# Two small transfers of an attention kernel, begun by ScalarE instead of SyncE from step 84 on

## The chip, the cores and the metric

The kernel runs on one core of a Trainium2 chip. The time is that of the device for one execution, in microseconds: 2188.83 us in the median of three runs before the change (2188.59 to 2190.87). Engines are named as the profile names them: PE is TensorE, PEld its weight loads, DVE is VectorE, ACT is ScalarE, POOL is GpSimd, SP is SyncE. Each engine works off its own queue of instructions in program order; an instruction that waits holds up everything behind it in that queue. A transfer (DMA) is begun by an instruction in the queue of some engine, and lands later.

## The reference, cut to what matters

```python
def _A_ref(x, wqkv, wo):                       # x: 1 x 2048 x 640
    H = 32; Dh = D // H; W = 256
    q, k, v = split((x @ wqkv).reshape(B, S, 3, H, Dh))
    scores = einsum("bhqd,bhkd->bhqk", q, k) * Dh ** -0.5
    mask = (idx[:, None] - idx[None, :] >= 0) & (idx[:, None] - idx[None, :] < W)
    p = softmax(where(mask, scores, -1e9))
    return einsum("bhqk,bhkd->bhqd", p, v).reshape(B, S, D) @ wo

def _B_ref(x, dft_seq_re, dft_seq_im, dft_hid_re, dft_hid_im):
    a = x @ dft_hid_re.T
    b = x @ dft_hid_im.T
    return dft_seq_re @ a - dft_seq_im @ b

x = x + _A_ref(_layernorm(x), A_wqkv, A_wo)
x = x + _B_ref(_layernorm(x), ...)
x = x + _A_ref(_layernorm(x), A_wqkv, A_wo)
x = x + _B_ref(_layernorm(x), ...)
```

Two attention layers with a window of 256 keys alternate with two Fourier layers. The change touches the attention layers alone, and both in the same way.

## The kernel before

An attention layer has 32 heads, taken in eight quads of four. Sixteen blocks of 128 positions times eight quads are 128 steps, which `heads` (L606) writes out in one order by hand. In step n it issues, for three different places in the sequence:

- **t**, place n: `t_pair` (L655) multiplies keys by queries for two heads at a time, so scores come out transposed, keys on the partitions (L659). The queries carry an extra row with the negated maximum of each query, and the keys a row of ones, so the maximum is subtracted within the product. `t_exp` (L663) takes the exponential on ScalarE (L669, twice a step: z = 0 and z = 1, two heads each), `t_mask` (L672) clears what lies outside the window on GpSimd (L675, L679).
- **s**, place n + 10: `s_head` (L626) makes the plain scores (L631), and VectorE adds the mask and takes each query's maximum (L636). For every four blocks `m_rows` (L641) transposes the maxima on TensorE (L644), ScalarE writes them negated to the tile `mt` (L647), and two transfers (L649) put them into the extra rows of the query tile `qp`. That happens in the steps 4k + 2, and the rows are wanted by L659 four steps later.
- **v**, place n - 1: `pv` (L685) multiplies the exponentials by the values (L694); a column of ones among the values gives the sum of each row. ScalarE copies the result to `ou` (L701). After every fourth block `finish` (L705) sends the row sums to the tile `sm` (L711) and the whole of `ou` to memory (L712), VectorE takes the reciprocals (L714), and they are sent to memory too (L717).

Scores live in banks of PSUM that are lent for a stretch of time by a plan (`borrow`, L139, and `borrow_pair`, L147, with the numbers HELD_T, HELD_S and HELD_PV). A bank that L669 hasn't read yet can't be written by the next L659, L631 or L694.

Between these products TensorE gets other work as filling: the projection of later quads (L257, then stored to `qk_d`, L524) and, when that is done, parts of the output product. Loads of head rows from `qk_d` into `kp` and `qp` (L594, twelve for each four blocks) are issued some four steps ahead of their use. Other loads are those of values (L621), of finished heads (L859) and their reciprocals (L865), of x (L951).

What matters for the change is who issues a transfer, and when. `post(delay, fn)` (L169) puts a function off by some ticks; there are two ticks a step (`tick`, L175, called at L829 after each z). A delay of 1 from within a half-step runs at that half-step's own end. So the two transfers of L649 are issued directly behind L647 in program order. The row sums have a delay of 2 in the first seven quads, which is the end of the next step's first half, behind that half's L669; in the last quad it is 1, directly behind L701. The reciprocal comes at a delay of 9, or 5 in the last quad. All transfers of the kernel are begun by SyncE, in the order in which they are issued.

Of the kernel before, what the change touches and what calls it, by code (L numbers as in the profile page):

```python
# [15 lines left out]
P = 128  # L16
# [5 lines left out]
NQ = H // 4  # L22
# [13 lines left out]
FIRST = 7  # L36
LATE = 9
BACK = 2
PACE = 0.65

STEP = 2.5
# [23 lines left out]
class Net:  # L65
# [89 lines left out]
    def next(self, name):  # L155
        i = self.turn.get(name, 0)
        self.turn[name] = i + 1
        tiles = getattr(self, name)[:3]
        return tiles[i % len(tiles)]
# [422 lines left out]
    def pack(self, quad, sb):  # L582
# [20 lines left out]
                    todo.append(lambda d=dst[b:b + 20, :, cols], src=src: put(d, src))  # L603
        return todo

    def heads(self, xsrc, xdst, hook):  # L606
        nc = self.nc
        qp = [t.rearrange("p (z s) -> p z s", z=2) for t in self.qp]
# [32 lines left out]
        def m_rows(quad, u, bank):  # L641
            m = mc.pop((quad, u))
            p = self.banks[:16, bank, 3 * P:]
            nc.tensor.transpose(p, m.rearrange("p z e j -> p (z e j)"), self.ident)  # L644
            mt = pool.tile([16, P], F32R, name="mt", tag="mt", bufs=1)
            yield
            nc.scalar.activation(mt, p, AF.Copy, scale=-1.0)  # L647
            for z in range(2):
                self.post(1, lambda z=z: nc.sync.dma_start(  # L649
                    qp[quad % 2][60:125:64, z, u * 512:(u + 1) * 512].bitcast(F32),  # L650
                    mt[8 * z:8 * z + 8, :].bitcast(F32)))

# [32 lines left out]
        def pv(quad, qb, bank):  # L685

            bk, at = qb // 4, qb % 4 * P
            if qb % 4 == 0:
                ous[quad, bk] = self.next("ou")
            for kb in range(max(qb - 2, 0), qb + 1):  # L690
                t = pt[quad, kb]
                vq = self.vq[(4 * quad + kb // 4) % 3]
                for h in range(4):
                    nc.tensor.matmul(  # L694
                        self.banks[32 * h:32 * h + 32, bank, :P],
                        vq[:, 96 * (kb % 4) + 21 * h:96 * (kb % 4) + 21 * h + 32],
                        t[:, h, (qb - kb) * P:(qb - kb + 1) * P],
                        start=kb == max(qb - 2, 0), stop=kb == qb,
                        tile_position=(0, 32 * h), skip_group_check=True)
            pt.pop((quad, qb - 2), None)  # L700
            nc.scalar.activation(ous[quad, bk][:, at:at + P], self.banks[:, bank, :P], AF.Copy)  # L701
            if qb % 4 == 3:
                finish(quad, bk)

        def finish(quad, bk):  # L705
            ou = ous.pop((quad, bk))
            sm = pool.tile([P, 16], F32, name="sm", tag="sm")
            rc = pool.tile([P, 16], F32, name="rc", tag="rc")
            cols = slice(bk * 512, (bk + 1) * 512)
            at = (2, 9, 11) if quad < NQ - 1 else (1, 5, 6)  # L710
            self.post(at[0], lambda: nc.sync.dma_start(sm, ou[0:P:32, :]))  # L711
            self.post(at[0], lambda: nc.sync.dma_start(  # L712
                self.od[4 * quad:4 * quad + 4, :, cols].rearrange("h r s -> (h r) s"), ou))
            self.post(at[1], lambda: nc.vector.reciprocal(out=rc, in_=sm))  # L714

            def store():
                nc.sync.dma_start(  # L717
                    self.rd[bk, 4 * quad:4 * quad + 4, :].rearrange("h (a b) -> (h a) b", b=16), rc)
                self.post(2 if quad < NQ - 1 else 0, lambda: self.stored.add((quad, bk)))
            self.post(at[2], store)  # L720
# [17 lines left out]
        def more():  # L738
# [5 lines left out]
            if not self.left:  # L744
                if self.part_t < NB - BACK:
                    self.now = self.out if self.ready_part() else None
                else:
                    self.now = self.rest if self.late_t < BACK and self.ready_late() else None
            return next(self.now, None) if self.now else None
# [26 lines left out]
        for step in range(-LEAD, steps + 1):  # L776
# [28 lines left out]
            for z in range(2):  # L805
                if 0 <= t < steps:
                    banks = self.borrow_pair(clock + AT_T[z], HELD_T)
                    t_pair(t // 16, t % 16, z, banks)
                if 0 <= s < steps:
                    for e, b in enumerate(self.borrow(clock + AT_S[z], *HELD_S)):  # L810
                        s_head(s // 16, s % 16, 2 * z + e, b)
                if z and (rows or 0 <= v < steps):
                    last, = self.borrow(clock + AT_PV, HELD_PV)
                m = m_rows(*rows, last) if z and rows else iter(())
                next(m, None)
                if 0 <= t < steps:
                    t_exp(t // 16, t % 16, z, banks)
                    t_mask(t // 16, t % 16, z)
                if self.heavy:
                    self.heavy.sort(key=lambda h: h[0] not in ROLES["m"])  # L820
                    self.relieve()
                if z:
                    if 0 <= v < steps:
                        pv(v // 16, v % 16, last)
                    for _ in m:
                        pass
                if z == 0 or t < -1 or t >= steps:
                    fill(nf)
                self.tick()  # L829
# [274 lines left out]
    def spend(self, us):  # L1104
        self.spent += us
        while self.spent >= PACE:
            self.spent -= PACE
            self.tick()
# [756 lines left out]
```

## Time and profile before

| | |
|---|---|
| median of three runs | 2188.83 us |
| the profiled execution | 2191.25 us |
| its span, first to last instruction | 2189.5 us |
| mean granted TensorE clock | 0.996 |
| transfers begun, all by SyncE | 1922 |
| of them L649 (`qp<-mt`, 4 KB each) | 128 |
| of them L711 (`sm<-ou`, 8 KB each) | 64 |
| steps 84 to 127, first attention layer | 390.65 to 531.2 us |
| steps 84 to 127, second attention layer | 1481.50 to 1623.7 us |

Times of steps are counted by the 256 executions of L669 in each layer, two a step, by their starts. In rows of the timeline the columns are: start, duration, engine, line, operation, what is written and read, how many are merged, and the engine's idle time before it with what ended it. "SPq" is SyncE's queue: a transfer's duration there is that of its issue, not of the data's way. A row of a stretch has start and end, its length, then for PE, PEld, DVE, ACT and POOL the busy time and the count, then the granted clock of TensorE, the share of the DMA engines that was busy, and GB/s. A row of waits reads: who waited, for whom, in total, how often, the longest.

### The profile page before, as it was taken

The page shows a single profiled execution, that of the slowest core. Times are in us where ns is not written, and L with a number is a line of the kernel's source. Part 1 is how long each engine was busy: PE and PEld are TensorE (multiplying, and loading weights), DVE is VectorE, ACT ScalarE, POOL GpSimd, SP SyncE. Part 2 cuts the span into 40 slices and gives each one's busy share as a digit, 9 for nine tenths or more (in the row PEclk, how much of TensorE's full clock was granted, in tenths as well). Part 3 has the DMA queues.
Part 4 walks back from the last instruction along what each step waited for, and adds up shares of the span by engine and source line. Part 5 has one row for each costly group of instructions (what it writes and reads, how often), then busy time and mean ns, then how long its engine had stood idle before and what let it go on. Part 6 is the DMA issues. An engine that isn't in the chain of part 4 may idle for free.

```text
span 2189.5 us, 48923 instructions
## 1 busy us (share of the span) xinstructions
PE 2119.5 (97%) x17872; PEld 1785.8 (82%) x17872; DVE 1600.5 (73%) x3931; ACT 1139.8 (52%) x2125; POOL 958.5 (44%) x1562
## 2 busy tenths in 40 slices
PE   7999999898999999999999999998999999999999
PEld 7987777677878888889999877776778888888899
DVE  6358888786897868786661588887867968687766
ACT  3117777656554545452341277776566645455332
POOL 3037776765513232332330376767655023241324
PEclk9999999999999999999999999999999999999999
DMA  5546666785566454656646566667855454546653
GB/s 183 175 156 190 199 180 210 213 222 172 200 192 188 129 183 140 212 185 200 205 156 177 161 187 196 186 204 208 216 165 180 141 187 135 166 152 209 225 166 126
DMA packets 227088, 398.40 MB, mean 182 GB/s; under 512 B 39968, under 2 KB 86560, under 8 KB 226848
## 3 DMA queue, kind: packets, MB, share of 16 engines
q1 hardware_dynamic: 226848, 395.28, 57.8%
q8 instruction: 141, 2.31, 0.5%
q14 instruction: 99, 0.81, 0.1%
HBM read 273.94 MB, written 120.06 MB: 180 GB/s over the span
## 4 chain that ended last, share of the span: by engine, by line
PE 79%; DVE 6%; DMA 4%; ACT 4%; POOL 3%; issue 2%; SPq 1%; ACTq 0%; DVEq 0%; POOLq 0%
PE banks L1415 29%; PE banks L239 15%; PE banks L257 12%; PE banks L694 6%; PE banks L659 5%; PE banks L1703 5%; PE banks L631 5%; DVE banks L636 1%; DMA qp<-qk_d 1%; ACT pt L669 1%; DVE qp L232 1%; PE banks L341 1%; DMA qk_d<-c 1%; ACT big L1038 1%; SPq L594 1%
## 5 line engine op out<-in xcount | busy, mean ns | idle before, releaser
L636 DVE CUSTOM_DVE_ANT_0 banks<-banks,mask 128x384 f32<-128x384 f32 (+2 forms) x1024 | 527.1, 556 | 121.4 <-PE banks L631 98.6
L669 ACT ACTIVATE pt<-banks 128x768 f32<-128x768 f32 (+2 forms) x512 | 393.5, 771 | 170.7 <-PE banks L659 59.8
L675 POOL TENSOR_SCALAR_AFFINE_SELECT pt<-pt 128x256 f32<-128x256 f32 x512 | 213.8, 418 | 220.3 <-ACT pt L669 201.6
L257 PE MATMUL banks<-big,wc 64*128 64x512 f32 x1920 | 271.4, 394 | 0.4 <-DVE pt L442 0.4
L659 PE MATMUL banks<-qp,kp 61*128 61x384 f32 (+2 forms) x1024 | 211.4, 382 | 24.2 <-DVE mc L636 17.0
L631 PE MATMUL banks<-kp,qp 60*128 60x384 f32 (+2 forms) x1024 | 206.9, 348 | 8.8 <-DVE mc L636 8.5
L694 PE MATMUL banks<-pt,vq 128*32 128x128 f32 x5760 | 211.2, 278 | 3.5 <-ACT pt L669 3.5
L257 PEld LDWEIGHTS banks<-big,wc 64*128 64x128 f32 x1920 | 187.3, 186 | 22.2 <-ACT x L544 1.3
L679 POOL TENSOR_SCALAR_AFFINE_SELECT pt<-pt 128x256 f32<-128x256 f32 x448 | 193.8, 433 | 0.0
L226 ACT ACTIVATE qp<-pt 128x512 fp32r<-128x512 f32 (+1 forms) x200 | 123.1, 625 | 129.3 <-DVE pt L1346 50.2
L232 DVE TENSOR_TENSOR qp<-pt,qp 128x512 fp32r<-128x512 f32 (+1 forms) x198 | 156.3, 797 | 40.9 <-ACT qp L226 39.3
L694 PEld LDWEIGHTS banks<-pt,vq 128*32 128x32 f32 x5760 | 142.2, 110 | 51.5 <-issue 36.2
L659 PEld LDWEIGHTS banks<-qp,kp 61*128 61x128 f32 x1024 | 108.6, 185 | 88.8 <-DVE mc L636 65.8
L1415 PE MATMUL banks<-qp,big 128*128 128x512 f32 x648 | 153.6, 391 | 0.1
L631 PEld LDWEIGHTS banks<-kp,qp 60*128 60x128 f32 x1024 | 124.7, 187 | 33.7 <-DVE mc L636 21.8
L1344 POOL TENSOR_TENSOR pt<-pt,pt 128x512 f32<-128x512 f32 x32 | 46.2, 1445 | 232.5 <-DMA pt<-c 146.0
L226 ACT ACTIVATE c<-pt 128x512 fp32r<-128x512 f32 x146 | 90.4, 625 | 108.2 <-POOL pt L1324 56.4
L636 DVE DVE_READ_ACCUMULATOR2_ANT mc<- 128x1 f32 x1024 | 144.3, 141 | 0.0
L1415 PEld LDWEIGHTS banks<-qp,big 128*128 128x128 f32 x648 | 120.8, 188 | 24.9 <-POOL qp L232 0.9
L232 DVE TENSOR_TENSOR c<-pt,c 128x512 fp32r<-128x512 f32 x144 | 116.6, 813 | 26.7 <-ACT c L226 24.1
L1415 PE MATMUL banks<-qp,xc 128*128 128x512 f32 x480 | 118.2, 394 | 3.6 <-DVE xc L232 2.1
L552 POOL CAST c<-x 128x512 fp32r<-128x512 f32 x64 | 38.9, 611 | 166.5 <-ACT x L544 162.3
(253 smaller groups left out, 4477.0 us busy)
## 6 DMA issues: line engine op xcount, KB each, us to landing
pt<-c SPq DMA_DIRECT2D x166, 512.0 KB
qk_d<-c SPq DMA_DIRECT2D x80, 512.0 KB
kp<-qk_d SPq DMA_DIRECT2D x384, 80.0 KB
qp<-qk_d SPq DMA_DIRECT2D x384, 80.0 KB
kp<-u_d SPq DMA_DIRECT2D x32, 640.0 KB
o_d<-ou SPq DMA_DIRECT2D x64, 256.0 KB
x_d<-x SPq DMA_DIRECT2D x48, 320.0 KB
v_d<-pt SPq DMA_DIRECT2D x16, 768.0 KB
```

The lines of the kernel that those rows point to most:

```text
L226: nc.scalar.activation(hi, src, AF.Copy, scale=-1.0 if neg else 1.0)
L232: (eng or nc.vector).tensor_tensor(out=lo, in0=src, in1=hi.bitcast(F32), op=OP.subtract)
L239: self.nc.tensor.matmul(p, x, y, start=n == 0, stop=n == last)
L257: self.nc.tensor.matmul(ps[a], x[r], y[r], start=half + i == 0, stop=half == 1 and i == n - 1, skip_group_check=True)
L631: nc.tensor.matmul(p, qp[quad % 2][b:b + 60, z, qb * P:(qb + 1) * P], kp[quad % 2][b:b + 60, z, k0 * P:(qb + 1) * P], start=True, stop=True)
L636: nc.vector.tensor_tensor_reduce(out=p, in0=p, in1=self.mask[:, 384 - n * P:], scale=1.0, scalar=NEG, op0=OP.add, op1=OP.max, accum_out=mc ...
L659: nc.tensor.matmul(self.banks[:, banks[e], :n * P], kp[quad % 2][b:b + 61, z, kb * P:(kb + 1) * P], qp[quad % 2][b:b + 61, z, kb * P:(kb + ...
L669: nc.scalar.activation(pt[quad, kb][:, 2 * z:2 * z + 2, :n * P], self.banks[:, b0:b1 + 1, :n * P], AF.Exp, scale=SCALE)
L675: nc.gpsimd.affine_select(out=t[:, :, 0:P], in_=t[:, :, 0:P], pattern=[[0, 2], [1, P]], compare_op=OP.is_ge, fill=0.0, base=0, channel_mul ...
L679: nc.gpsimd.affine_select(out=t[:, :, 256:384], in_=t[:, :, 256:384], pattern=[[0, 2], [-1, P]], compare_op=OP.is_gt, fill=0.0, base=0, ch ...
L694: nc.tensor.matmul(self.banks[32 * h:32 * h + 32, bank, :P], vq[:, 96 * (kb % 4) + 21 * h:96 * (kb % 4) + 21 * h + 32], t[:, h, (qb - kb) ...
L1415: nc.tensor.matmul(self.banks[:, bk, :], p, b[q], start=start and m == 0, stop=stop and last and m == 2, skip_group_check=True)
```

## The change

The transfers at L649 (negated maxima) and L711 (row sums) are begun by ScalarE when they are issued in steps 84 to 126, and by SyncE otherwise. `self.step` is the step in which the posted function runs. The transfer of `ou` to memory (L712), that of the reciprocals (L717) and all loads stay on SyncE. What is transferred, the tiles and the order of issue are the same.

```diff
+BUSY = 84
...
+    def quick(self):
+
+        return self.nc.scalar if BUSY <= self.step < 16 * NQ - 1 else self.nc.sync
...
             nc.scalar.activation(mt, p, AF.Copy, scale=-1.0)
             for z in range(2):
-                self.post(1, lambda z=z: nc.sync.dma_start(
+                self.post(1, lambda z=z: self.quick().dma_start(
                     qp[quad % 2][60:125:64, z, u * 512:(u + 1) * 512].bitcast(F32),
                     mt[8 * z:8 * z + 8, :].bitcast(F32)))
...
             at = (2, 9, 11) if quad < NQ - 1 else (1, 5, 6)
-            self.post(at[0], lambda: nc.sync.dma_start(sm, ou[0:P:32, :]))
+            self.post(at[0], lambda: self.quick().dma_start(sm, ou[0:P:32, :]))
             self.post(at[0], lambda: nc.sync.dma_start(
                 self.od[4 * quad:4 * quad + 4, :, cols].rearrange("h r s -> (h r) s"), ou))
```

## The prediction

> **What bounds the kernel now.** I read the page first (shares of the engines, then the chain of waits), then the timeline of steps 84 to 127 of both attention layers, then the waits and stretches of those steps. Steps are counted by L669, which runs twice in each. The page says that TensorE sets the end: it is busy for 97% of the span and makes 79% of the chain of waits, ScalarE is busy for half of the span and makes 4% of the chain.
>
> ```profile
> span 2189.5 us, 48923 instructions
> PE 2119.5 (97%) x17872; PEld 1785.8 (82%) x17872; DVE 1600.5 (73%) x3931; ACT 1139.8 (52%) x2125; POOL 958.5 (44%) x1562
> PE 79%; DVE 6%; DMA 4%; ACT 4%; POOL 3%; issue 2%; SPq 1%; ACTq 0%; DVEq 0%; POOLq 0%
> ```
>
> So a gain has to come out of the 3% in which TensorE stands still or runs slowly, and a loss comes from any ScalarE delay that TensorE has to wait for. The first layer's timeline around step 97 shows what there is to win. The columns are start, duration, engine, line, operation, what it writes and reads, count, and in brackets the idle time before it and who ended it.
>
> ```profile
> 416.10 0.44 PE L659 MATMUL banks<-qp,kp 61*128 61x384 f32 x2
> 421.64 0.25 ACT L647 ACTIVATE mt<-banks 16x128 fp32r<-16x128 f32 x1
> 421.95 1.43 SPq L594 DMA_DIRECT2D qp<-qk_d  x3
> 424.26 0.61 SPq L711 DMA_DIRECT2D sm<-ou  x1
> 426.69 0.45 PE L659 MATMUL banks<-qp,kp 61*128 61x384 f32 x2
> 429.62 0.25 DVE L714 RECIPROCAL rc<-sm 128x16 f32<-128x16 f32 x1 [2.47 <-DMA sm<-ou]
> 430.30 1.08 SPq L649 DMA_DIRECT2D qp<-mt  x2
> 430.45 0.44 PE L631 MATMUL banks<-kp,qp 60*128 60x384 f32 x2 [1.64 <-DVE mc L636]
> 432.96 0.69 PE L659 MATMUL banks<-qp,kp 61*128 61x384 f32 x2 [1.71 <-DMA qp<-mt]
> 438.65 0.69 PE L659 MATMUL banks<-qp,kp 61*128 61x384 f32 x2
> 451.75 0.45 PE L659 MATMUL banks<-qp,kp 61*128 61x384 f32 x2
> ...
> 433.70:440.80 7.10, 7.10 (x65) 6.02 (x66) 4.15 (x13) 2.85 (x5) 2.00 (x6) 0.59 0.83 203
> ```
>
> The reader is to see two late transfers. The negated maxima were finished at 421.89 and their transfer was begun at 430.30, 8.4 us later, because it stood behind SyncE's other work; TensorE waited 1.71 us for it. The row sums belong to step 92, their transfer could have begun in step 93 (which starts at 416.10) and was begun at 424.26; VectorE stood 2.47 us for it at L714, and TensorE then 1.64 us for VectorE. The last row, a stretch, adds that TensorE's granted clock was 0.59 right behind the two stops. The second layer repeats it with a longer first stop:
>
> ```profile
> 1516.35 0.60 SPq L711 DMA_DIRECT2D sm<-ou  x1
> 1517.55 0.44 PE L659 MATMUL banks<-qp,kp 61*128 61x384 f32 x2
> 1522.63 0.25 DVE L714 RECIPROCAL rc<-sm 128x16 f32<-128x16 f32 x1 [4.62 <-DMA sm<-ou]
> 1523.45 0.44 PE L631 MATMUL banks<-kp,qp 60*128 60x384 f32 x2 [3.79 <-DVE mc L636]
> 1525.95 0.69 PE L659 MATMUL banks<-qp,kp 61*128 61x384 f32 x2 [1.71 <-DMA qp<-mt]
> 1531.65 0.46 PE L659 MATMUL banks<-qp,kp 61*128 61x384 f32 x2
> ```
>
> **What can be won.** L659 at 438.65 opens step 99 and at 451.75 step 103: 13.10 us for four steps, 3.28 a step. Steps 97 and 98 together took 438.65 - 426.69 = 11.96 us in the first layer and 1531.65 - 1517.55 = 14.10 in the second. Against 2 x 3.28 = 6.55 that is 5.4 and 7.55 us too much, slow clock included: 12.95 us. With the change both transfers begin about 7 to 8 us earlier, and even at the slowest landing shown (1516.35 to 1522.63, 6.3 us) they arrive before they are asked for. What is late next are the head rows that L594 begins at 421.95, wanted by L631 in step 98, which would now start near 426.69 + 3.28 = 429.97. At 5.4 us of landing (424.26 to 429.62) from the last issue, 421.95 + 1.43 = 423.4, they come at 428.8, about a microsecond ahead; in the second layer it is tighter. I take 0.5 us off in each layer: **11.9 us won**. The bounds are 0 (a new wait takes the whole place) and 12.95.
>
> **What is moved.** Rows of maxima come in steps 86, 90, ... 118, nine a layer, two transfers each: 36 issues in both layers. Row sums are finished in steps 84, 88, ... 124: eleven a layer, 22 issues. The last one (step 128) stays on SyncE. In all 58 of the 192 such transfers move. Their price on SyncE:
>
> ```profile
> L649 SPq DMA_DIRECT2D qp<-mt x128: 503/532/814, 143.9 to 1599.5; - x128
> L711 SPq DMA_DIRECT2D sm<-ou x64: 582/607/624, 177.2 to 1627.2; - x64
> ```
>
> ScalarE begins no transfer in this trace, so its price is bounded by these rows: 503 to 814 ns each for the maxima, and from below by nothing at all where an issue can run beside an activation. I take SyncE's medians, as it is the same transfer. A pair then holds ScalarE for 1.1 us (the row at 430.30 shows 1.08), and since it has to wait for L647's own result it can't run beside it. Behind it in ScalarE's queue stand the next exponentials, L669, and for those TensorE waits, since they free the score banks:
>
> ```profile
> 399.87 0.25 ACT L647 ACTIVATE mt<-banks 16x128 fp32r<-16x128 f32 x1
> 400.19 1.75 ACT L669 ACTIVATE pt<-banks 128x768 f32<-128x768 f32 x2
> 401.05 0.18 PEld L631 LDWEIGHTS banks<-kp,qp 60*128 60x128 f32 x1 [0.16 <-ACT pt L669]
> 438.97 0.25 ACT L647 ACTIVATE mt<-banks 16x128 fp32r<-16x128 f32 x1
> 439.39 0.81 ACT L669 ACTIVATE pt<-banks 128x768 f32<-128x768 f32 x1 [0.17 <-PE banks L659]
> 440.96 0.35 PE L631 MATMUL banks<-kp,qp 60*128 60x384 f32 x2
> 506.64 0.79 ACT L669 ACTIVATE pt<-banks 128x768 f32<-128x768 f32 x1
> 507.52 0.60 PEld L694 LDWEIGHTS banks<-pt,vq 128*32 128x32 f32 x24 [0.22 <-ACT pt L669]
> ```
>
> In step 86 (the first three rows) the exponential starts 0.07 us behind L647, and TensorE already waits for its end: a delay of 1.1 us goes straight through, 1.05 us. In step 98 it ends at 440.20 and TensorE asks for its bank at 440.96, so of the delay (1.15 - 0.17 us) 0.76 are free and some 0.2 are paid. In step 118 there is no room again. Read in this way, the nine steps fall into five like step 86 (86, 90, 94, 102, 118) and four like step 98 with 0.6 to 0.8 us of room (98, 106, 110, 114), of which I take 0.33 us each. That is 5 x 1.05 + 4 x 0.33 = 6.6 us a layer, **13.1 us paid** for the maxima; at 814 ns each it would be 18 x 0.56 = 10 us more.
>
> The row sums of steps 84 to 112 are begun behind the first exponential of the next step, whose producer is long done: 607 ns beside 771 ns of L669. I cost them at nothing; the cover is that exponential, and without it they cost up to 16 x 0.6 = 10 us, less the gaps. In steps 116, 120 and 124 the issue stands right behind the copy L701, with L669 behind it.
>
> ```profile
> L669 ACT ACTIVATE pt<-banks 128x768 f32<-128x768 f32 (+2 forms) x512 | 393.5, 771 | 170.7 <-PE banks L659 59.8 <-PE banks L631 47.1 <-POOL pt L675 39.0
> 523.59 0.28 ACT L701 ACTIVATE ou<-banks 128x128 f32<-128x128 f32 x1
> 524.59 1.49 ACT L669 ACTIVATE pt<-banks 128x768 f32<-128x768 f32 x2
> 525.43 0.59 PEld L694 LDWEIGHTS banks<-pt,vq 128*32 128x32 f32 x24 [1.33 <-ACT pt L669]
> ```
>
> In step 124 TensorE waits for those exponentials, so about 0.5 us of the 0.61 is paid; for steps 120 and 116 I take 0.3 and 0.15: 0.95 us a layer, **1.9 us**.
>
> SyncE loses 58 issues, some 32 us of its queue. Beside the waits above, these steps of the first layer show one more of TensorE on a transfer:
>
> ```profile
> PE banks L659 <- DMA qp<-qk_d: 0.6, 1, 0.6
> ```
>
> So a freer SyncE is worth next to nothing elsewhere, and I count nothing for it. **The sum:** -11.9 + 13.1 + 1.9 = +3.1 us. It is made against the profiled execution, 2191.25 us (span 2189.5); the median shown is 2188.83, so I carry the difference over: **2191.9 us**, from 2186 to 2198 by the uncertainty of the paid share.
>
> **The rivals.** *ScalarE's delays are mostly absorbed: faster.* For it speaks that ScalarE has room over the stretch of steps 96 to 111 and that TensorE often waits for VectorE there anyway, so an exponential that is late may only use up another wait:
>
> ```profile
> 424.60:483.20 58.60, 51.83 (x764) 42.67 (x764) 44.33 (x151) 32.24 (x60) 35.05 (x75) 0.94 0.81 218
> PEld banks L659 <- DVE mc L636: 14.2, 30, 2.0
> ```
>
> Against it: most of those 30 waits are as short as a weight load's own turn, and VectorE's work itself waits for the L631 that the late bank holds up. If a quarter of the 15 us is paid, the change is -11.9 + 3.75 = -8.2 us: 2180.7.
>
> *The two issuing engines get in each other's way: slower.* When L647 ends at 421.89, SyncE begins three transfers in 1.43 us, one behind the other. If only one engine's transfer can be prepared at a time, each issue on ScalarE waits for the rest of SyncE's, up to 1.43 / 3 = 0.48 us, on average 0.24: 36 x 0.24 = 8.6 us, less what the four roomy steps hide, 7.5 us. It decides once a pair takes over 1.4 us on ScalarE. 2199.4. The Trainium skill (Perfetto Trace Analysis, "DMA Instruction — HWDGE (DVE, Sync)") speaks for it: the generator of descriptors is locked for one issuing engine at a time, and the wait for the lock lies within the recorded duration. No run here shows two engines issuing.
>
> *The stalls only change their name: slower still.* Transfers wait for unrelated ones to land:
>
> ```profile
> SPq L594 <- DMA big<-x: 3.1, 3, 1.1
> ```
>
> A load of head rows waits here for a load of x, so completions are counted in turns. If ScalarE's transfers take turns with SyncE's, ScalarE's queue stands until some large load has landed, with the exponentials behind it. At half of the longest such wait for each of the 18 pairs, 18 x 0.55 = 10 us: about 2202. Against it: the wait came three times in 140 us.
>
> **Chances.** Forecast 0.45, absorbed 0.30, in each other's way 0.16, turns 0.09. A measurement of this kernel tells some 0.2% from no change, here 4.4 us: under 2184.4 is faster, over 2193.2 slower. The forecast's own range lies on both sides of that (0.03 faster, 0.27 same, 0.15 slower); the first rival is faster but for 0.01, the others are slower. Faster 0.32, same 0.28, slower 0.40. The range goes from 2179 to 2203, which leaves out the lower end of the first rival and the upper end of the last.
>
> **What would show it.** Right: no bracket "DMA sm<-ou" before L714 and none "DMA qp<-mt" before L659 in steps 97 and 98, steps of about 3.3 us there, a full granted clock; L649 on ScalarE's queue at 0.5 us each, right behind L647; waits of TensorE for "ACT pt L669" up by about 1 us in steps 86, 90, 94, 102 and 118. The forecast is wrong if a pair holds ScalarE far longer or shorter than 1.1 us, if these waits don't grow, or if step 98 waits for L594's rows instead.

## The result, and the profile after

The changed kernel takes 2240.97 us in the median of four runs (2231.76 to 2246.61) against 2188.71 us (2186.26 to 2190.87): a ratio of 1.0232, 95% interval 1.0214 to 1.0249. It is slower by 52 us; 2191.9 us had been forecast, with 2203 as the upper end. Code lines ahead of the new function are one further down (L594 is now L595), those behind it five: L621 is L626, L631 and L636 are L636 and L641, L649 is L654, L659 is L664, L669 is L674, L701 is L706, L711 and L712 are L716 and L717, L714 is L719, L717 is L722, L859 and L865 are L864 and L870, L951 is L956.

From the page of the changed kernel, the span, the busiest engines and the shares of the chain of waits:

```profile
span 2244.9 us, 48855 instructions
PE 2146.6 (96%) x17872; PEld 1800.3 (80%) x17872; DVE 1603.1 (71%) x3931; ACT 1139.6 (51%) x2125; POOL 958.6 (43%) x1562
PE 60%; DVE 6%; DMA 6%; ACT 4%; issue 3%; POOL 3%; SPq 1%; ACTq 0%; DVEq 0%; POOLq 0%
```

ScalarE's busy time is unchanged (1139.6 against 1139.8 us: issues do not count as busy), and TensorE's share of the chain has fallen from 79% to 60%. The loss is in the steps in which transfers were moved. Steps 84 to 126 of both layers as stretches, of the kernel before and then of the changed one; columns as in the prediction:

```profile
390.04:528.15 138.11, 124.38 (x1869) 98.07 (x1865) 101.60 (x334) 89.33 (x163) 98.08 (x208) 0.98 0.71 203
1480.88:1620.70 139.82, 124.42 (x1870) 97.82 (x1866) 102.25 (x334) 89.37 (x163) 98.21 (x208) 0.98 0.72 196
```

```profile
390.62:556.38 165.76, 137.79 (x1869) 105.45 (x1865) 102.53 (x334) 89.01 (x163) 96.35 (x208) 0.89 0.60 173
1510.96:1674.67 163.71, 134.47 (x1869) 103.16 (x1865) 103.30 (x334) 88.85 (x163) 96.83 (x208) 0.92 0.59 170
```

They are 27.65 and 23.89 us longer, 51.5 us of the 55.4 by which the spans differ. The same matmuls take 272.3 us in place of 248.8, at a granted clock of 0.89 and 0.92 in place of 0.98: 23.5 us of the loss is TensorE being busy for longer, the other 28 us is TensorE standing.

The two stops that the change could remove are gone. The timeline of the changed kernel around steps 97 and 98:

```profile
425.60 0.59 ACTq L716 DMA_DIRECT2D sm<-ou  x1
...
431.42 1.09 ACTq L654 DMA_DIRECT2D qp<-mt  x2
...
438.76 0.25 DVE L719 RECIPROCAL rc<-sm 128x16 f32<-128x16 f32 x1
...
438.90 0.69 PE L664 MATMUL banks<-qp,kp 61*128 61x384 f32 x2
...
442.81 0.44 PE L664 MATMUL banks<-qp,kp 61*128 61x384 f32 x2 [0.33 <-DVE mc L641]
...
446.44 0.45 PE L664 MATMUL banks<-qp,kp 61*128 61x384 f32 x2 [0.31 <-DVE mc L641]
```

No bracket names "DMA sm<-ou" or "DMA qp<-mt" any more, and steps 97 and 98 take 446.44 - 438.90 = 7.54 us together, where they took 11.96. (In the second layer it is 7.53 for 14.10.) What is new stands in the waits of SyncE's queue, a view of the changed kernel: who waited, for whom, in total, how often, the longest.

```profile
SPq L595 <- DMA qp<-mt: 39.9, 11, 4.8
SPq L722 <- DMA sm<-ou: 19.0, 4, 5.3
SPq L870 <- DMA sm<-ou: 10.0, 2, 5.1
SPq L595 <- DMA sm<-ou: 8.9, 2, 5.6
SPq L956 <- DMA sm<-ou: 8.0, 2, 4.4
SPq L626 <- DMA qp<-mt: 6.2, 2, 3.6
```

With one more of 0.3 us these are 24 waits of 3.8 us on average, 92.3 us in all; before there was none on these two transfers. Several of the waiting lines have nothing to do with what they wait for: L870 loads the reciprocals of heads finished long ago, L956 loads x, L626 loads values. The timeline of steps 101 and 102 of the first layer shows how TensorE comes to pay:

```profile
439.70 0.60 ACTq L716 DMA_DIRECT2D sm<-ou  x1
...
451.14 0.52 SPq L864 DMA_DIRECT2D x<-o_d  x1
...
453.85 0.59 ACTq L716 DMA_DIRECT2D sm<-ou  x1
...
456.56 0.51 SPq L870 DMA_DIRECT2D rr<-r_d  x1
...
457.81 1.90 SPq L717 DMA_DIRECT2D o_d<-ou  x1
...
462.32 0.28 ACT L706 ACTIVATE ou<-banks 128x128 f32<-128x128 f32 x1 [6.06 <-DMA o_d<-ou]
...
462.65 0.68 PE L664 MATMUL banks<-qp,kp 61*128 61x384 f32 x1 [4.32 <-ACT ou L706]
...
466.75 0.69 PE L664 MATMUL banks<-qp,kp 61*128 61x384 f32 x2
```

SyncE is ready for L870 at 451.66, but L870 goes at 456.56, 4.9 us later: 2.7 us after ScalarE began an unrelated transfer of row sums. Behind L870 stands L717, which stores the finished heads of step 96; their row sums had been begun at 439.70, 18 us earlier. ScalarE's copy L706 has to overwrite that tile, waits 6.06 us for the store to land, and TensorE's banks stay taken for 4.32 us. Step 102 (456.22 to 466.75) takes 10.5 us instead of 3.3, at a granted clock of 0.75. The same wait of L706 comes in step 102 of the second layer and in step 110 of both; these four steps hold 26 of the 51.5 us. ScalarE had seven such waits, none before:

```profile
ACT ou L706 <- DMA o_d<-ou: 29.2, 7, 6.1
```

### The profile page after: what moved, and what is told of

Read it like the earlier page. It is cut to its first block, busy times and chain, and to the rows that moved or that the text cites. A ratio compares the mean times of both kernels' runs of the same rounds, so it can differ in the third digit from the quotient of the medians.

```text
span 2244.9 us, 48855 instructions
## 1 busy us (share of the span) xinstructions
PE 2146.6 (96%) x17872; PEld 1800.3 (80%) x17872; DVE 1603.1 (71%) x3931; ACT 1139.6 (51%) x2125; POOL 958.6 (43%) x1562
## 4 chain that ended last, share of the span: by engine, by line
PE 60%; DVE 6%; DMA 6%; ACT 4%; issue 3%; POOL 3%; SPq 1%; ACTq 0%; DVEq 0%; POOLq 0%
PE banks L1420 28%; PE banks L240 11%; PE banks L258 6%; PE banks L1708 5%; PE banks L699 4%; PE banks L664 3%; PE banks L636 3%; ACT pt L674 1%; DMA o_d<-ou 1%; DVE banks L641 1%; DMA rr<-r_d 1%; DVE qp L233 1%; ACT big L1043 1%; ACT qp L227 1%; DMA sm<-ou 1%
## 5 line engine op out<-in xcount | busy, mean ns | idle before, releaser
L641 DVE CUSTOM_DVE_ANT_0 banks<-banks,mask 128x384 f32<-128x384 f32 (+2 forms) x1024 | 528.4, 556 | 169.2 <-PE banks L636 138.2
L674 ACT ACTIVATE pt<-banks 128x768 f32<-128x768 f32 (+2 forms) x512 | 392.0, 771 | 173.9 <-PE banks L664 54.3
L664 PE MATMUL banks<-qp,kp 61*128 61x384 f32 (+2 forms) x1024 | 215.3, 389 | 35.8 <-ACT ou L706 16.0
L636 PE MATMUL banks<-kp,qp 60*128 60x384 f32 (+2 forms) x1024 | 216.4, 356 | 21.9 <-ACT pt L674 16.9
L699 PE MATMUL banks<-pt,vq 128*32 128x128 f32 x5760 | 219.1, 285 | 6.8 <-ACT pt L674 6.2
L664 PEld LDWEIGHTS banks<-qp,kp 61*128 61x128 f32 x1024 | 110.9, 189 | 103.7 <-DVE mc L641 60.6
L699 PEld LDWEIGHTS banks<-pt,vq 128*32 128x32 f32 x5760 | 147.0, 112 | 57.0 <-issue 36.6
L636 PEld LDWEIGHTS banks<-kp,qp 60*128 60x128 f32 x1024 | 128.2, 191 | 52.7 <-ACT pt L674 26.0
L641 DVE DVE_READ_ACCUMULATOR2_ANT mc<- 128x1 f32 x1024 | 145.3, 142 | 0.0
L706 ACT ACTIVATE ou<-banks 128x128 f32<-128x128 f32 x256 | 71.5, 279 | 104.3 <-PE banks L699 65.1
```

Source lines behind the costliest of these rows:

```text
L636: nc.tensor.matmul(p, qp[quad % 2][b:b + 60, z, qb * P:(qb + 1) * P], kp[quad % 2][b:b + 60, z, k0 * P:(qb + 1) * P], start=True, stop=True)
L641: nc.vector.tensor_tensor_reduce(out=p, in0=p, in1=self.mask[:, 384 - n * P:], scale=1.0, scalar=NEG, op0=OP.add, op1=OP.max, accum_out=mc ...
L664: nc.tensor.matmul(self.banks[:, banks[e], :n * P], kp[quad % 2][b:b + 61, z, kb * P:(kb + 1) * P], qp[quad % 2][b:b + 61, z, kb * P:(kb + ...
L674: nc.scalar.activation(pt[quad, kb][:, 2 * z:2 * z + 2, :n * P], self.banks[:, b0:b1 + 1, :n * P], AF.Exp, scale=SCALE)
L699: nc.tensor.matmul(self.banks[32 * h:32 * h + 32, bank, :P], vq[:, 96 * (kb % 4) + 21 * h:96 * (kb % 4) + 21 * h + 32], t[:, h, (qb - kb) ...
```

## The theory and its rivals

In the trace every transfer's record names the semaphore on which its landing is counted. There are eight of them for SyncE and ScalarE together, with 240 or 241 of the 1922 transfers each, and they are dealt out in turn when the kernel is built, in the order in which all transfers were planned. A transfer waits until the one that had its semaphore last, eight places ahead, has landed. As long as SyncE begins everything, that one is always older in its own queue. **Theory T:** in the built program ScalarE's transfers of steps 84 to 113 have a place 12 to 28 earlier in this order than they had on SyncE, as the turns of the semaphores in both traces show; from step 114 on the difference is at most 4. On the chip SyncE then gets to the transfer eight places further on, often before ScalarE has begun its own, and the whole queue of SyncE stands until ScalarE's has been begun and has landed. The trace of the changed kernel bears this out: in all 24 waits the waiting transfer has the same semaphore as the ScalarE transfer that it waits for (105 for L870 at 456.56 and L716 at 453.85), and in 15 of them SyncE was ready before ScalarE had begun its own. Rivals: **R**, ScalarE is held by its issues and TensorE pays for late exponentials; **L**, a second issuing engine disturbs the first; **N**, it is a true dependence on the data that was moved.

## The experiments

| run | what differs from the kernel before | median, us | before on the same chip | ratio (95%) |
|---|---|---|---|---|
| e1 | only row sums begun by ScalarE | 2218.31 | 2191.03 | 1.0134 (1.0110 to 1.0157) |
| e2 | only maxima begun by ScalarE | 2210.11 | 2191.03 | 1.0090 (1.0071 to 1.0109) |
| e3 | nothing moved, ScalarE held by copies | 2200.24 | 2191.03 | 1.0044 (1.0026 to 1.0061) |
| e4 | all 58 begun by GpSimd | 2197.47 | 2191.03 | 1.0033 (1.0021 to 1.0044) |
| e5 | nothing moved, 58 useless transfers on ScalarE | 2254.30 | 2189.56 | 1.0290 (1.0269 to 1.0310) |
| e6 | GpSimd begins them in steps 92 to 98 | 2186.25 | 2189.56 | 0.9984 (0.9972 to 0.9996) |
| e7 | SyncE alone, four loads of x spread out | 2190.73 | 2189.56 | 1.0002 (0.9989 to 1.0014) |
| e8 | the change, ScalarE's turns as SyncE had them | 2218.41 | 2188.70 | 1.0128 (1.0109 to 1.0147) |
| e9 | the change, turns some seven places earlier | 2204.07 | 2188.70 | 1.0072 (1.0052 to 1.0091) |
| e10 | GpSimd begins three transfers a layer | 2185.86 | 2188.70 | 0.9986 (0.9973 to 0.9999) |

**e1 and e2: one half of the change each.** In e1 L654 is begun by `nc.sync` again, in e2 L716.

```diff
-                self.post(1, lambda z=z: self.quick().dma_start(
+                self.post(1, lambda z=z: nc.sync.dma_start(
```

> Only the 22 transfers of row sums are begun by ScalarE; those of the maxima stay on SyncE. Theory T (taken turns): in the changed kernel SyncE's queue stands until ScalarE's transfers have landed, 44 us of it in steps 84 to 127 of the first layer and 48 us in the second; in the rows of SyncE's waits about 22 and 24 us of this are on 'sm<-ou'. Then this kernel loses roughly half of what the change loses: 2200 to 2220 us, with loads of x, head rows and reciprocals (L594, L865, L951) waiting 3 to 5 us for 'sm<-ou'. Rival R (ScalarE is held by its issues): the row sums hold it for 0.6 us beside other work, so the time is 2180 to 2190 us, below or at that of before, since the stop at L714 in step 97 goes. Rival L (two issuing engines block each other): 22 of 58 issues, 2190 to 2208 us, and the issues themselves last longer than 0.6 us.

> Only the 36 transfers of the negated maxima are begun by ScalarE; the row sums stay on SyncE. T: the other half of SyncE's waits remains (some 22 to 24 us a layer on 'qp<-mt'), 2200 to 2225 us, with kp<-qk_d and vq<-v_d, which have nothing to do with the maxima, waiting for 'qp<-mt'. R: nearly all of the loss comes from the pairs of 1.1 us between L647 and L669, so 2230 to 2245 us here. L: two thirds of the loss, 2215 to 2230 us, and issues longer than 0.53 us.

Both halves lose, 27 and 19 us. The row sums alone, which stand behind an exponential and should cost ScalarE nothing, lose the more: against R. SyncE's waits for "sm<-ou" are 45 us in e1 (L595, L654, L956, L525), those for "qp<-mt" 38 us in e2; the largest group of each:

```profile
SPq L595 <- DMA sm<-ou: 20.5, 6, 5.7
```

```profile
SPq L595 <- DMA qp<-mt: 37.5, 12, 6.0
```

**e3: ScalarE's time without its transfers.** SyncE begins everything; ScalarE does two copies of 128 columns at the place of each issue.

```diff
+    def hold(self, n):
+        for _ in range(n):
+            self.nc.scalar.activation(self.pad, self.pad, AF.Copy)
...
+                if BUSY <= self.step < 16 * NQ - 1:
+                    self.post(1, lambda: self.hold(2))
```

> SyncE begins every transfer as before; ScalarE does two (row sums) or four (maxima) copies of 128 columns at the places where the change has its issues, some 0.28 us each, so that it is held for the same 0.6 and 1.1 us without beginning anything. T: the loss of the change does not need ScalarE's time; at most the 15 us of the prediction's own terms are paid, 2189 to 2204 us, and the stops in steps 97 and 98 stay. R: as slow as the change without the 12 us of its gain, 2240 to 2255 us. L: 2189 us, no more than a few us off.

9 us, within T's bound, far from R's. Steps 84 to 126 as stretches of this run, then the stretches of its steps 97 and 98:

```profile
388.87:529.70 140.83, 126.23 (x1870) 98.36 (x1866) 102.17 (x334) 103.19 (x221) 97.29 (x208) 0.98 0.70 200
1482.34:1624.43 142.09, 127.61 (x1869) 99.44 (x1865) 102.12 (x334) 103.26 (x221) 97.35 (x208) 0.97 0.69 196
...
429.98:437.47 7.49, 6.82 (x82) 5.37 (x78) 5.09 (x18) 4.45 (x10) 2.60 (x7) 0.91 0.76 205
1522.65:1531.26 8.61, 8.10 (x81) 6.36 (x77) 4.99 (x17) 4.56 (x10) 2.60 (x7) 0.74 0.73 214
```

One expectation was wrong: most of the stops of steps 97 and 98 goes although SyncE begins the late transfers as before. The held exponentials make TensorE arrive at step 97 later, 429.98 - 388.87 = 41.1 us after the start of step 84 where it was 36.7, while SyncE begins the row sums and the maxima 33.3 and 39.4 us after that start, nearly as before (34.2 and 40.3). So the price of ScalarE's time is what these stretches lost, with what the stops gave back added: (140.83 - 138.11) + (11.96 - 7.49) = 7.2 us in the first layer and (142.09 - 139.82) + (14.10 - 8.61) = 7.8 in the second, 15.0 us. This goes by one profiled execution of each kernel; the two lie 6.0 us apart, where the medians lie 9.2 apart, so the price is known to a few us.

**e4: the same transfers begun by GpSimd.** Its transfers are counted on other semaphores than SyncE's and ScalarE's (111 to 118 in this trace, where SyncE's are 100 to 105, 107 and 109).

```diff
-        return self.nc.scalar if BUSY <= self.step < 16 * NQ - 1 else self.nc.sync
+        return self.nc.gpsimd if BUSY <= self.step < 16 * NQ - 1 else self.nc.sync
```

> The same 58 transfers are begun by GpSimd in place of ScalarE, at the same places in the order of issue. Its transfers count their completions on semaphores of their own, apart from those which SyncE's and ScalarE's share. T: SyncE no longer waits for any of the 58; the stops of steps 97 and 98 go and nothing takes their place unless GpSimd's masks become late: 2172 to 2192 us. R: ScalarE isn't held, so the same, 2172 to 2192 us. L (any second issuing engine disturbs SyncE's): slower than before, 2200 to 2240 us. If GpSimd's own issues last over a microsecond, its masks L675 and L679 come late and TensorE's L694 waits for them: up to 58 x 1 us, 2190 to 2230 us, without any wait of SyncE.

SyncE has no wait for the moved transfers here, and 6 us are lost where the change loses 52, which speaks against L and for T. The stops are gone, at full clock (first two rows, the stretches of steps 97 and 98). The 6 us are more than T's bound allows; the issues on GpSimd ahead of its masks are a likely cause, which no run tests (the groups of GpSimd: busy time and mean ns):

```profile
430.02:436.78 6.76, 6.10 (x81) 4.76 (x77) 5.03 (x18) 3.93 (x8) 3.63 (x9) 1.00 0.86 217
1522.40:1529.16 6.76, 6.08 (x81) 4.76 (x77) 5.03 (x18) 3.95 (x8) 3.64 (x9) 1.00 0.96 205
```

```profile
L654 POOL DMA_DIRECT2D qp<-mt x36 | 20.0, 558 | 1.8 <-ACT mt L652 1.2 <-issue 0.5
L716 POOL DMA_DIRECT2D sm<-ou x22 | 16.1, 731 | 1.0 <-DVE seen L264 0.4
```

**e5: transfers that nobody needs.** SyncE begins all that it did before; ScalarE sends the same tiles to two unused ones.

```diff
             self.post(at[0], lambda: nc.sync.dma_start(sm, ou[0:P:32, :]))
+            self.post(at[0], lambda: self.again() and nc.scalar.dma_start(self.sx, ou[0:P:32, :]))
```

> SyncE begins all transfers of before, the row sums and the maxima too; ScalarE begins 58 more behind them, which carry the same tiles to two tiles that nobody reads. Theory T (completions are counted in turns, in the planned order, so SyncE's next transfer in the turn waits until ScalarE's has landed): it does not matter that nobody needs them, SyncE waits some 70 to 100 us for 'mx<-mt' and 'sx<-ou', and the time is 2230 to 2260 us. Rival N (the loss comes with the real data, for instance a true dependence on the rows of qp or on sm): only ScalarE's time is paid, as in the run with copies in their place, 2195 to 2206 us.

N falls: 65 us are lost with no needed transfer moved, and SyncE waits 75 us for the useless ones: 31 waits, each for a transfer that had its own semaphore before it. The four largest of these waits, in which loads of head rows (L597 here) and of finished heads (L869), and transfers of maxima (L655), wait for tiles that nothing reads:

```profile
SPq L597 <- DMA sx<-ou: 19.4, 8, 3.5
SPq L597 <- DMA mx<-mt: 15.6, 5, 3.8
SPq L655 <- DMA sx<-ou: 11.2, 4, 3.7
SPq L869 <- DMA mx<-mt: 7.9, 2, 4.3
```

**e8 and e9: the turn alone.** Each engine's instructions are those of the changed kernel, in the same order. Only the planned place of ScalarE's transfers differs: in e8 behind the transfer of SyncE that is written just ahead of it, in e9 six to eight places earlier than that in steps 84 to 110. SyncE's own order is pinned by edges of the same kind. The edge fixes the order in the plan; nothing waits for it on the chip. The lines of e8:

```diff
+        last = next(i for i in reversed(self.nc.cur_bb.bb.instructions)
+                    if i.engine == mybir.EngineType.SP)
+        d = self.nc.scalar.dma_start(dst, src)
+        self.tc.add_manual_dep(d.ins, last.name, mybir.DependencyInfo(
+            mybir.DependencyClass.NoSync, mybir.DependencyReason.DATA))
```

> The changed kernel, with the same instructions in the same order on each of the five engines; only the place that ScalarE's transfers take in the planned order of all transfers is another: each is planned behind the transfer of SyncE that is written just ahead of it, so that it takes the turn (and the counter) that it had when SyncE began it, 12 to 28 places later than in the changed kernel. Theory T: SyncE's 92 us of waits for these transfers fall under 15 us and the time falls by over 25 us, to 2190 to 2215 us. What is left above the time of before is ScalarE's own price (9 us in the run with copies) and waits of ScalarE for a counter where SyncE is late, steps 93 to 98 first. Rival M (anything else in beginning transfers on ScalarE): nothing that the engines do has changed, so 2235 to 2250 us as in the changed kernel.

> As the run before it, but planned behind the transfer that SyncE begins some seven places earlier, about half of the way to the changed kernel. T: SyncE's waits for ScalarE's transfers lie between the two, 10 to 50 us, ScalarE's own waits for a counter are shorter, and the time is 2190 to 2225 us. M: 2235 to 2250 us.

This shows the cause of most of the loss. With the same instructions in the same order, e8 loses 23 us and e9 37 us less than the change; by rival M of the expectations neither could. SyncE's waits for the moved transfers fall from 92 us to these, in e8 and then in e9, and in none of them was SyncE ready before ScalarE had begun its own (the line named is that of a helper, L63 or L620):

```profile
SPq L63 <- DMA qp<-mt: 19.2, 11, 3.6
```

```profile
SPq L63 <- DMA qp<-mt: 16.5, 17, 2.7
SPq L63 <- DMA sm<-ou: 6.5, 4, 2.6
```

e8 lies 3 us over T's range, and its 19 us are over the 15 expected. It is slower than e9 though SyncE waits no longer. With late turns ScalarE stands for SyncE's transfers. The start of step 86 in e8, from the timeline:

```profile
396.67 1.26 ACTq L620 DMA_DIRECT2D sm<-ou  x1
397.98 0.74 ACT L227 ACTIVATE big<-we 128x640 fp32r<-128x640 f32 x1 [3.50 <-DMA x<-o_d]
```

ScalarE sits idle for 3.50 us. The view puts all of it down to a load of finished heads, but the wait just ahead of the issue is for semaphore 100, on which a load of values that SyncE began at 393.64 landed at 396.58; the issue then takes 1.26 us. Step 86 takes 7.5 us where it took 3.0 (6.7 in the second layer), which is 8 of the 15 us by which the stretches of steps 84 to 126 in e8 are longer than in e9. So the coupling costs in both directions, and of the three places tried the one between is cheapest.

**e6, e7 and e10: where the stops come from, and a faster kernel.** e6 and e10 are e4 with the window cut down to steps 92 to 98 and to steps 93 and 94; e7 is the kernel before with the loads of x spread:

```diff
-            self.load_y(range(AHEAD_X))
+            self.load_y(range(1))
+            for t in range(1, AHEAD_X):
+                self.defer(t, lambda t=t: self.load_y([t]))
```

> GpSimd begins the moved transfers in steps 92 to 98 only, six in a layer. If the stops of steps 97 and 98 are the late transfers and nothing else, they go and GpSimd's six issues of 0.6 to 0.7 us cost 1 to 2 us a layer: 2191 - 12 + 3, so 2179 to 2185 us. If they are a backlog of SyncE's queue that comes out at the next transfer that is wanted, the stop turns up again in steps 99 to 104 and the time stays at 2187 to 2195 us.

> SyncE begins everything, as before; the four loads of x (L951) that before began together at 420.12 to 421.91, right ahead of the late transfers, are begun one a step instead. If the stops of steps 97 and 98 come from these loads, which hold four of the counters for 7 us or so, the row sums and the maxima are begun 2 to 4 us earlier and half or more of the 12 us goes: 2178 to 2186 us. If the backlog has another source, 2189 to 2193 us.

> GpSimd begins only the three late transfers of a layer: the row sums in step 93 and the two of maxima in step 94; everything else is SyncE's. If these three alone make the stops of steps 97 and 98, the time is that of the run in which GpSimd begins six, less one or two us for the three issues saved: 2182 to 2187 us. If the other three were needed too, the gain is lost: 2188 to 2192 us.

e7 changes the time by nothing that shows, and its steps 97 and 98 still take 12.19 and 11.30 us (11.96 and 14.10 before): the four loads of x right ahead of the late transfers are not the main cause. e6 and e10 are faster than the kernel before, by 3.3 and 2.8 us, with intervals just clear of 1. The time of e6 lies between the two ranges expected for it; its steps 97 and 98 take 8.14 and 8.42 us, and the stop does not turn up again in steps 99 to 104. e10's stretches of steps 97 and 98 are 8.70 and 8.21 us:

```profile
428.94:437.64 8.70, 8.24 (x82) 6.37 (x78) 4.99 (x17) 4.06 (x8) 2.60 (x7) 0.73 0.83 238
1518.51:1526.72 8.21, 7.68 (x83) 5.97 (x79) 5.04 (x18) 4.05 (x8) 2.94 (x8) 0.79 0.80 242
```

Moving these three is enough, then, but of the 12.95 us that stood in the stops 3.26 + 5.89 = 9.2 come off there, and 2.8 us arrive in the median. In the profile of e10 step 96 is 1.9 and 1.0 us longer than before, and steps 84 to 126 together are 5.4 us shorter; what takes the rest stays open. So does the source of the backlog itself.

## Why the prediction was wrong

**The issues on ScalarE: right.** They were to take 0.5 us each for the maxima and 607 ns for the row sums. In the changed kernel (minimum, median, maximum in ns):

```profile
L654 ACTq DMA_DIRECT2D qp<-mt x36: 515/523/591, 400.7 to 1651.5; - x36
L716 ACTq DMA_DIRECT2D sm<-ou x22: 550/598/1111, 394.2 to 1669.3; - x22
```

**What ScalarE's time costs: right.** The forecast's 15.0 us stand against 15.0 in e3, and the steps behind 86, 90, 94, 102 and 118, forecast at 1.05 us each, are 1.05, 1.12, 1.56, 0.85 and 1.21 us longer in e3's first layer. That the sums agree to the tenth is luck. e3's time rises by 9 us only (6 to 13 by the interval), since the same delay takes most of the stops away.

**The stops of steps 97 and 98: right in place, nearly in size.** 11.9 us were to go, 4.42 + 6.57 = 11.0 went. The full granted clock that was to be a sign of it didn't come: it was 0.86 in these two steps of the first layer. That this is a gain of the change's own was wrong: in e3 a delay of TensorE ahead of step 97 takes 4.47 + 5.49 = 10.0 us off them with no transfer moved.

**"So a freer SyncE is worth next to nothing elsewhere, and I count nothing for it": this step failed.** SyncE did not become freer. It lost 58 issues, some 32 us, and gained 92 us of waits for the engine that had taken them. The mechanism stands in the prediction as the third rival, turns of completion, but on the wrong queue and too small: ScalarE's queue was to stand, for 0.55 us in each of 18 pairs, 10 us, taken from the longest wait of that kind in the trace of before (1.1 us), and it got a chance of 0.09 because that wait came three times in 140 us. Both numbers come from a queue whose turns were all its own. There the transfer eight places ahead has always been begun, and only the end of its landing is left to wait for. With a second engine in the turn it may not have been begun at all, as in 15 of the 24 waits: 3.8 us a wait, 24 times, on the queue through which all other loads and stores go. The working is then -11.0 + 15.0 + 48 us, the last term being what the stretches of the changed kernel show beyond the other two (51.5 - 4.0). e9 shows 37 us of it directly, by moving the turn alone; for the other 11 us no run stands by itself, though SyncE still waits 23 us in e9.

**The rival of two engines in each other's way: not seen.** It needed pairs of over 1.4 us, and the pair at 431.42 takes 1.09 us. The Trainium skill (Perfetto Trace Analysis, "DMA Instruction — HWDGE (DVE, Sync)") puts the wait for the lock within the recorded duration. The rows above are no longer than SyncE's own, but for single ones like the 1111 ns. Of the 58 issues on ScalarE 24 began while SyncE was issuing: their medians are 524 ns (maxima) and 598 ns (row sums), against 520 and 599 where SyncE issued nothing at the time, and the 1111 ns is one of the latter. So such a lock has no visible price here.

**The range** ended at 2203 because the highest case was priced at 2202. The side was the likeliest of the three by the chances (slower, 0.40), and it came out by luck: the reason that decided it had a chance of 0.09. The size was missed by a factor of seventeen (52 us for 3.1).

## What to carry to other kernels

Before a transfer is given to another engine, ask on which semaphore its landing is counted, which transfer has that semaphore next, and whether that one's engine gets there first: two queues that share a few semaphores in turn (eight here) are tied to each other within that many places, and the faster one loses its lead. Look in the waits of the queue that the work was taken from, for lines that wait for transfers they have no business with. A delay elsewhere can take away a stop behind a late transfer, as in e3, and the wait can move to the step ahead, as in e10, so the length of the stop isn't the gain.

## What the runs showed of the hardware

Stops seem to be paid twice. In the stretches of the changed kernel the same matmuls took 23.5 us more, at a granted clock of 0.89 and 0.92 instead of 0.98; in e9, with fewer stops, it was 0.96 and 0.95 (the rows below). That the standing lowers the clock is read from such pairs of traces; no run tests it alone.

```profile
387.87:531.89 144.02, 128.48 (x1870) 99.63 (x1866) 102.15 (x334) 89.21 (x163) 97.94 (x208) 0.96 0.72 199
1487.20:1631.92 144.72, 128.51 (x1870) 99.58 (x1867) 102.17 (x334) 89.00 (x163) 97.74 (x208) 0.95 0.69 193
```

GpSimd takes longer than ScalarE to begin the row sums, 718 against 598 ns in the median, and little longer for the maxima, 556 against 523 ns.
